# One NeuronCore, attention and two feed-forward layers: the order of 3,095 planned operations read from a table

## The chip, the core and the metric

The kernel runs on one core of a Trainium2 chip. The metric is the device time of one execution in microseconds (us); lower is better. The engines go by the names of the profile: PE is TensorE's matmuls, PEld its weight loads, DVE is VectorE, ACT is ScalarE, POOL is GpSimd, SP is SyncE, which here only issues transfers (DMAs). Each engine runs its own instructions in order, and waits on semaphores for the others.

## What is computed

Attention with rotary positions over 2 batches, 8 heads, 576 positions and 64 channels; its output (1152 tokens of 512) goes through a layer of width 2048 and then through four experts of width 1024 that are all computed and mixed by given probabilities.

```python
q_rot, k_rot = rotate(q), rotate(k)              # per head, 576 x 64
scores = q_rot @ k_rot.T / 8; scores -= max
attn = exp(scores); attn /= sum + 1e-9
x = (attn @ v)                                   # as 1152 x 512
h = x @ w_in                                     # 512 x 2048
g = where(h >= 1, h, where(h <= -1, 0, (h + 1)**2 / 4))
x = g @ w_out                                    # 2048 x 512
for e in range(4):
    out += p[:, e:e+1] * (relu(x @ w1[e]) @ w2[e])   # 512 x 1024, 1024 x 512
```

All is in float32. The kernel splits each operand of a product into a high and a low part that TensorE takes fast, and adds three products (high x high, high x low, low x high).

## The kernel before

The kernel first describes its work as *operations*, each of one engine, by calls of `op(engine, ns, prio, fn, reads, writes, bufs, ...)`: `fn` issues the instructions (one to twenty), `reads` and `writes` name what must come before it, `bufs` are the ring buffers that it occupies. Operations get a number in the order in which they are described, 0 to 3094. `Plan.order` then puts them in one sequence, and the kernel issues them in that sequence; the engine's own order is what is left of it when one looks at that engine alone. The compiler's framework derives the semaphores from the data. `order` keeps a model of the time: when each engine is free (`free`), when an operation's inputs are there (`ready`), when a ring has a buffer. `est(o)` is the earliest start of an operation in this model. Before, the next operation is found greedily: on each engine the one with the smallest start, or among those that can start within `ahead` = 42.6 ns of the engine's being free the one with the smallest priority; then the engine that can start first. Priorities are a base by pair and tile plus one offset per kind of operation (`CFG["o"]`). Where the model sees TensorE idle for more than `fill` = 272 ns, up to 190 us, `order` puts *filler* matmuls into the hole (tile `warm`, L1328): products of the identity that nobody reads. Operation 0 is a placeholder: 1000 ns of TensorE in the model, with no instruction.

**Attention** goes through eight *pairs* of heads, n = 0 to 7 (four per batch). For each: k, q and v are loaded by SyncE in three parts each (positions 0 to 255, 256 to 511, and the last 64; tiles `rawk`, `rawq`, `RV`); `rope` rotates k and q in three steps (L981, L985, L989) on VectorE or GpSimd; `split_h` and `split_l` make high and low parts (`hlk`, `hlq`; L1028 is the low part); TensorE transposes them (`pstk`, `pstq`), ScalarE copies them to `K` and `Q`; a transfer makes the copy K2 with its halves exchanged. In the first pair q and k are worked on in segments, and VectorE and ScalarE make K and K2 from transposes of their own (`k_first`, L1085, L1092).

Then nine *tiles* of 128 rows of scores, s = 0 to 8, in `tile_step`: scores into `sc` (L1162, four matmuls; eight for s = 8, L1172), a ring of two PSUM buffers; the maximum `nm` on VectorE (L1179); the exponential `E` on ScalarE (L1184), which frees `sc`; four transposes of E into `pt` (L1197), a ring of three; and a copy of them (`PT`). For each half of the tiles, `tails` transposes the rest (`pu`), `av` multiplies with v (L1273, 20 matmuls in the records), the reciprocal of the sums goes over DRAM to all partitions (`r`, `rb`, `rt`, `rdram`, `rbs`), and the product `avx` is split into `XH` and `XL`.

**The first layer** (phases 2 and 1) has four *chunks* c of 512 columns, each with three blocks b of 384 tokens and four units: `in_unit` (PSUM tile `pi`, L520) with its activation, and `out_unit` (`po`, L574). The first units of chunk 0 may run within attention. Its weights come in 1 MB blocks of 64-bit numbers (`wrawa`, L378) and are converted on ScalarE and VectorE (`w_split`, L423 to L438, one quarter of a block at a time; later `w_split2`). **The experts** (eight chunks; `in2`, L776; `out2`, L813) follow, with converted weights (`conv1`, `conv2`).

Of the kernel before, what the change touches and what calls it, by code (L numbers as in the profile page):

```python
# [41 lines left out]
    },  # L42
}


def _f32_of_bits(b):
# [90 lines left out]
class Plan:  # L137
# [38 lines left out]
    def order(self):  # L176
        prio = {o: o.prio for o in self.ops}
        free, ready, left = {}, {}, {}
        for o in self.ops:
            free.setdefault(o.eng, self.START.get(o.eng, 0.0))  # L180
            ready.setdefault(o.eng, [])
            left[o.phase] = left.get(o.phase, 0) + 1
            if o.need == 0:
                ready[o.eng].append(o)
        out = []
        n = len(self.ops)
        ahead = CFG["ahead"]

        cols = [0.0] * 1000
        heat, heat_to = CFG["fill"], CFG["fill_to"]  # L190
        port = [0.0, None]
        mode = [0]
        queue = 0.0

        def est(o):
            t = max(free[o.eng], o.ready)
            if o.port:
                t = max(t, port[0])
            if o.phase == 1 and left.get(0, 0):
                return None  # L200
            for b in o.bufs:
                if b.slot is None:
                    r = b.ring
                    if r.ordered and b.idx != len(r.live):
                        return None
                    i = len(r.live) - r.bufs
                    if i >= 0:
                        if r.live[i].left:
                            return None
                        t = max(t, r.live[i].end)  # L210
            if o.eng == "PE" and o.mode != mode[0]:
                t += self.ENTER if o.mode else self.LEAVE
            return t

        while len(out) < n:
            best = None
            for e, rl in ready.items():
                c = None
                for o in rl:
                    t = est(o)  # L220
                    if t is None:
                        continue
                    key = (max(t, free[e] + ahead), prio[o], o.seq)
                    if c is None or key < c[0]:
                        c = (key, t, o)
                if c and (best is None or (c[1], c[0][1]) < (best[1], best[0][1])):
                    best = c
            if best is None:
                raise RuntimeError("no order")
            _, t, o = best  # L230
            if o.eng == "PE" and heat and t - free["PE"] > heat and free["PE"] < heat_to:
                g0 = free["PE"]
                early = g0 < CFG["warm_to"]
                r = self.filler[early]
                i = len(r.live) - r.bufs
                ok = i < 0 or not r.live[i].left
                if ok and i >= 0:
                    g0 = max(g0, r.live[i].end)
                k = int(g0 // self.TICK)
                cyc = 228.0 if g0 < CFG["warm_to"] or cols[k - 1] >= self.FULL else 430.0  # L240
                if CFG["rule"] and g0 > CFG["warm_to"]:
                    ok = ok and cols[k] + CFG["rule"] * (self.TICK * (k + 1) - g0) < self.FULL
                cnt = int((t - g0 - 40) // cyc)
                slow = 0
                if k == 0:
                    slow = min(12, int((t - g0 - 40) // 430.0))
                    cnt = slow + int((t - g0 - 40 - slow * 430.0) // cyc)
                if ok and cnt > 0:
                    f = self.fill(cnt, early)
                    b = f.bufs[0]  # L250
                    b.slot = len(r.live)
                    r.live.append(b)
                    f.start, f.ns = g0, cnt * cyc + slow * (430.0 - cyc)
                    b.end, b.left = g0 + f.ns + (0.0 if early else self.LAT["PE"]), 0
                    for z in range(cnt):
                        at = g0 + z * cyc + min(z, slow) * (430.0 - cyc)
                        cols[int(at // self.TICK)] += 512
                    free["PE"] = g0 + f.ns
                    out.append(f)
                    n += 1  # L260
                    continue
            ready[o.eng].remove(o)
            left[o.phase] -= 1
            o.start = t
            ns = o.ns
            if o.eng == "PE":
                if t > free["PE"] + 20 and o.mode == mode[0] and ns:
                    ns += self.STALL
                mode[0] = o.mode
                k = int(t // self.TICK)  # L270
                if k == 0 or cols[k - 1] < self.FULL:
                    ns *= 1.96
                m = min(1.0, (self.TICK * (k + 1) - t) / ns)
                cols[k] += o.cols * m
                cols[k + 1] += o.cols * (1 - m)
            end = t + ns
            lat = o.lat
            if o.dma:
                queue = max(queue + o.dma, end + lat)
                lat = queue - end  # L280
            free[o.eng] = end
            if o.port:
                x = port[1]
                o.behind = x if x is not None and o.eng == "POOL" and x.eng == "DVE" else None
                port[:] = end, o
            for b in o.bufs:
                if b.slot is None:
                    b.slot = len(b.ring.live)
                    b.ring.live.append(b)
                b.left -= 1  # L290
                b.end = max(b.end, end + lat + self.LAT[o.eng])
            for x in o.outs:
                x.need -= 1
                x.ready = max(x.ready, end + lat + (130.0 if x.eng == o.eng and o.eng != "PE" else
                                                      0.0 if x.eng == o.eng else self.LAT[o.eng]))
                if x.need == 0:
                    ready[x.eng].append(x)
            out.append(o)
        return out
# [1216 lines left out]
```

## Time and profile before

| | us |
|---|---|
| median of 3 runs (lowest, highest) | 745.22 (745.02, 747.79) |
| the profiled execution | 743.66 |
| its span, first to last instruction | 741.9 |
| PE busy in the span | 731.7 |
| DVE busy | 537.3 |
| ACT busy | 352.4 |
| POOL busy | 90.7 |

The profile is of one execution. Busy time is the time in which at least one instruction of an engine runs; for TensorE the ends of matmuls are modelled and successive ones overlap, so that a busy TensorE need not be at its peak. Idle time is followed back to the instruction or transfer that ended it. The profiled execution's own time holds 1.8 us outside its span.

### The profile page before, as it was taken

Reading aid. Unit: us, or ns where it says so; the run is one execution under the profiler, and the core shown is the slowest. Engines: PE = TensorE matmul, PEld = TensorE weight load, DVE = VectorE, ACT = ScalarE, POOL = GpSimd, SP = SyncE. Lnnn points to the kernel's source line nnn. Section 1 sums busy time; section 2 is a strip of 40 time slices with the busy share of each in tenths; the row PEclk is TensorE's granted clock in tenths of the full one; section 3 lists DMA queues with packets and bytes.
Section 4 is the critical chain, followed back from the end, with each engine's and each line's share of the span. In section 5 each row is a group of like instructions: output and inputs, shape, how many; then the busy total and the mean of one; then the engine's idle time right before and its main releaser. Section 6 shows DMA issues by size and latency. Waiting matters only on the chain.

```text
span 741.9 us, 11798 instructions
## 1 busy us (share of the span) xinstructions
PE 731.7 (99%) x4551; PEld 664.1 (90%) x4551; DVE 537.3 (72%) x1054; ACT 352.4 (48%) x801; POOL 90.7 (12%) x88
## 2 busy tenths in 40 slices
PE   8999999999999999999999999999999999999998
PEld 6877778879999999999998889998899989999896
DVE  6789899799999943225898586684866749668462
ACT  4887788776776554435533332331433314333110
POOL 2874433000000021222300000000000000000000
PEclk9999999999999999999999999999999999999999
DMA  6344434223362400000103110111011110111002
GB/s 185 93 118 129 125 98 141 90 74 123 121 215 83 151 0 1 1 2 1 57 1 114 57 47 11 58 57 57 12 46 57 57 57 18 41 58 57 1 29 100
DMA packets 38872, 50.86 MB, mean 69 GB/s; under 512 B 7640, under 2 KB 22560, under 8 KB 38816
## 3 DMA queue, kind: packets, MB, share of 16 engines
q1 hardware_dynamic: 38126, 49.61, 21.4%
q8 instruction: 36, 0.59, 0.3%
q10 hardware_dynamic: 690, 0.49, 0.2%
q14 instruction: 20, 0.16, 0.1%
HBM read 43.34 MB, written 2.40 MB: 62 GB/s over the span
## 4 chain that ended last, share of the span: by engine, by line
PE 90%; DVE 4%; ACT 2%; DMA 2%; POOL 1%; issue 1%; SPq 0%; DVEq 0%; POOLq 0%
PE po L813 27%; PE q L776 23%; PE po L574 13%; PE pi L520 13%; PE av L1273 5%; PE sc L1162 4%; PE pt L1197 3%; ACT E L1184 1%; PE sc L1172 1%; DVE nm L1179 1%; DMA rawq<-in_q_dram 1%; PE pu L1223 1%; DVE tsa L785 1%; DMA rawk<-in_k_dram 1%; PE pstk L1045 1%
## 5 line engine op out<-in xcount | busy, mean ns | idle before, releaser
L785 DVE TENSOR_TENSOR tsa<-q,tsa 128x256 f32<-128x256 f32 (+1 forms) x224 | 93.3, 448 | 32.9 <-PE q L776 32.4
L813 PE MATMUL po<-w,ct 128*128 128x512 f32 (+1 forms) x328 | 99.1, 384 | 0.0
L828 DVE SCALAR_TENSOR_TENSOR ACC<-po,ptile,ACC 128x512 f32<-128x512 f32 (+1 forms) x64 | 46.8, 739 | 65.8 <-PE po L813 65.8
L813 PE MATMUL po<-w,hid1h 128*128 128x512 f32 x256 | 79.0, 390 | 0.0
L813 PEld LDWEIGHTS po<-w,ct 128*128 128x128 f32 x328 | 60.5, 188 | 11.7
L813 PE MATMUL po<-w,tsb 128*128 128x512 f32 (+1 forms) x164 | 63.0, 384 | 0.0
L1184 ACT ACTIVATE E<-sc,nm 128x576 f32<-128x576 f32 x72 | 53.7, 748 | 13.1 <-DVE nm L1179 9.6
L1179 DVE TENSOR_REDUCE nm<-sc 128x1 f32<-128x576 f32 x72 | 52.6, 751 | 8.8 <-PE sc L1162 3.8
L813 PEld LDWEIGHTS po<-w,hid1h 128*128 128x128 f32 x256 | 47.6, 188 | 9.4
L665 ACT CAST w<-wrawa 128x512 fp32r<-128x512 f32 x32 | 18.4, 617 | 67.5 <-PE po L813 63.3
L813 PE MATMUL po<-w,hid1l 128*128 128x512 f32 x128 | 50.0, 390 | 0.0
L541 ACT ACTIVATE hb<-pi,half_t 128x384 f32<-128x384 f32 x48 | 27.8, 578 | 46.3 <-PE pi L520 46.2
L759 ACT ACTIVATE ct<-tsa 128x320 fp32r<-128x320 f32 x64 | 28.9, 471 | 42.7 <-DVE tsa L785 42.7
L1162 PE MATMUL sc<-K,Q 128*128 128x288 f32 x256 | 46.3, 311 | 2.3 <-ACT E L1184 2.1
L545 DVE SCALAR_TENSOR_TENSOR hb<-hb,pi 128x384 f32<-128x384 f32 x48 | 26.3, 550 | 28.0 <-ACT hb L543 17.9
L759 ACT ACTIVATE hid1h<-tsa 128x256 fp32r<-128x256 f32 x64 | 25.4, 418 | 36.8 <-DVE tsa L785 36.7
L1162 PEld LDWEIGHTS sc<-K,Q 128*128 128x128 f32 x256 | 35.9, 188 | 7.6 <-ACT E L1184 5.7
L1197 PE MATMUL pt<-ident,E 128*128 128x128 f32 x288 | 38.4, 274 | 0.3 <-ACT K L1050 0.3
L788 ACT COPY tsa<-q 128x256 f32<-128x256 f32 (+1 forms) x32 | 12.7, 398 | 51.7 <-PE q L776 51.6
L586 DVE TENSOR_TENSOR ACC<-po,ACC 128x384 f32<-128x384 f32 x36 | 20.0, 555 | 23.9 <-PE po L574 23.9
L813 PEld LDWEIGHTS po<-w,tsb 128*128 128x128 f32 x164 | 30.8, 188 | 6.2
L776 PE MATMUL q<-XH,w00l 128*128 128x256 f32 (+1 forms) x120 | 35.5, 296 | 0.0
(234 smaller groups left out, 1961.2 us busy)
## 6 DMA issues: line engine op xcount, KB each, us to landing
wrawa<-in_moe_w_dram SPq DMA_DIRECT2D x16, 1024.0 KB, 5.9
wrawa<-in_moe_w_in_dram SPq DMA_DIRECT2D x5, 1024.0 KB
wrawa<-in_moe_w_out_dram SPq DMA_DIRECT2D x5, 1024.0 KB, 5.1
K<-K SPq DMA_DIRECT2D x14, 304.0 KB, 3.4
ta<-in_moe_w_in_dram SPq DMA_DIRECT2D x3, 1024.0 KB
ta<-in_moe_w_out_dram SPq DMA_DIRECT2D x3, 1024.0 KB, 4.9
rawk<-in_k_dram SPq DMA_DIRECT2D x16, 128.0 KB, 3.6
RV<-in_v_dram SPq DMA_DIRECT2D x16, 128.0 KB, 2.4
```

The costliest lines, as they stand in the source:

```text
L520: nc.tensor.matmul(ps()[:, 0:384], w[:, kt * P:(kt + 1) * P], x[:, kt, cols], start=(kt == 0 and m == 0), stop=(kt == 3 and m == 2))
L574: nc.tensor.matmul(ps()[:, 0:N], lh, rh, start=(kt == 0 and m == 0), stop=(kt == 3 and m == 2))
L759: op("ACT", act_ns(n, port) + 20, pr, lambda: nc.scalar.activation(hv(0), src(), AF.Relu), rk + gates[0], [hk], bufs, phase=1)
L776: nc.tensor.matmul(ps()[:, 0:n], w[x][:, kt, a * P:(a + 1) * P], r[y][:, kt, :], start=(kt == 0 and m == 0), stop=(kt == 1 and m == 2))
L785: nc.vector.tensor_tensor(ct(a, j), psv(), ct(a, i), op=ALU.add)
L813: nc.tensor.matmul(ps()[:, 0:f1 - f0], x[y], w[z][:, f0:f1], start=(kt == 0 and m == 0), stop=(kt == 3 and m == 2))
L828: op("DVE", 65 + 1.17 * (f1 - f0), pr, lambda acc=acc, ps=ps, t=t, f0=f0, f1=f1: nc.vector.scalar_tensor_tensor(acc(), ps()[:, 0:f1 - f0], ...
L1162: nc.tensor.matmul(sc()[:, a, 0:288], lh, KK()[:, c0:c0 + 288], start=(x == 0), stop=(x == 1))
L1179: op("DVE", 665, g0 + O["max"], lambda: nc.vector.tensor_reduce(nm(), pv(), axis=AX.XY, op=ALU.max, negate=True), [sc], [nm], [sc, nm])
L1184: nc.scalar.activation(Et()[:, o0:o0 + 576].rearrange("p (a c) -> p a c", a=2), pv(), AF.Exp, bias=nm(), scale=1.0, accum_out=sm()[:, s:s ...
L1197: nc.tensor.transpose(ps()[:, t * P:(t + 1) * P], Et()[:, c0 + t * P:c0 + (t + 1) * P], ident)
L1273: nc.tensor.matmul(pa()[64 * j:64 * j + 64, 0:N], lh, rh, start=(t == 0), stop=(t == 4))
```

## The change

The greedy choice is replaced by a table, `ORDER`: all 3,095 numbers in the sequence in which they are to be issued. `order` takes the first number that is left, asks `est` for its start, and goes on as before: fillers are still put in where its model sees a hole. `est` gets one more rule: a GpSimd operation that follows a VectorE operation on their shared port starts one VectorE latency (125 ns) later. Nothing else is changed: the offsets stay in the file and have no effect on the sequence any more.

To read the first numbers: 1, 2 and 9 are SyncE's loads of pair 0's k (last 64 positions, first part, second part), 10 its load of q's second part; 3 and 4 load the rotation tables on ScalarE's queue, 5 and 6 parts of q; 45, 46 and 47 are the three rotation steps of k's second segment, 48 to 50 those of q's; 14 to 16 those of k's first; 57 is VectorE's copy to K2 of its second segment; 58 is the split of q's second segment on ScalarE; 868 is the load of the first weight block (1 MB); 133, 134 and 135 load pair 1's k; 142 and 143 are two rotation steps of it on VectorE, 144 the third on GpSimd; 148 and 149 its high and low part; 152, 156 and 162 its transposes; 62, 67, 72 the scores of tiles 0, 1 and 3 of pair 0 (the third to be computed is tile 3), 63 the maximum of tile 0.

```diff
--- before.py
+++ after.py
+ORDER = """
+3 9 45 4 10 1 48 46 49 6 2 47 15 14 5 37 38 51 50 16 18 17 39 19 20 53 58 12 868 7 59 54 40 22 41 23 28 133 8 134 135
+142 143 11 21 144 55 32 24 29 52 33 31 25 136 26 56 30 27 60 138 61 57 137 62 148 42 44 149 145 146 34 238 63 35 36 67
+0 68 43 162 64 72 152 139 69 163 77 73 156 153 65 74 157 78 158 239 240 82 247 75 79 83 147 76 242 66 87 84 150 248 88
+151 243 241 250 80 110 111 85 86 81 92 112 70 108 89 166 93 113 97 13 71 94 109 114 98 154 343 164 159 102 155 90 99
+160 161 167 251 165 116 91 103 141 252 344 168 104 123 105 120 249 253 124 121 254 169 172 115 125 126 100 177 173 347
+174 345 122 257 101 178 261 258 95 353 346 263 262 179 127 348 352 182 267 268 175 271 449 176 448 96 183 255 256 170
+187 106 184 171 107 185 180 213 192 117 188 189 186 181 197 128 356 214 354 259 264 265 269 193 118 140 355 198 357
+260 129 358 451 215 450 194 266 199 216 217 270 119 912 359 869 452 130 202 195 196 203 458 218 207 204 190 208 209
+372 219 220 362 272 870 913 363 373 457 273 228 191 221 210 459 225 131 453 226 205 229 366 227 274 277 206 368 555
+360 367 230 278 554 282 283 361 231 279 211 200 275 212 222 284 276 201 287 374 375 364 244 365 292 871 288 369 371
...
+3065 3063 3066 3064 3067 3068 3071 3069 3072 3070 3073 3074 3077 3075 3078 3076 3079 3080 3083 3081 3084 3085 3082
+3086 3089 3087 3090 3088 3091 3092 3093 3094
+"""
@@ -189,13 +318,15 @@
         cols = [0.0] * 1000
         heat, heat_to = CFG["fill"], CFG["fill_to"]
         port = [0.0, None]
+        table = [self.ops[int(x)] for x in ORDER.split()]
         mode = [0]
         queue = 0.0
 
         def est(o):
             t = max(free[o.eng], o.ready)
             if o.port:
-                t = max(t, port[0])
+                behind = port[1] is not None and o.eng == "POOL" and port[1].eng == "DVE"
+                t = max(t, port[0] + (self.LAT["DVE"] if behind else 0.0))
             if o.phase == 1 and left.get(0, 0):
                 return None
             for b in o.bufs:
@@ -214,7 +345,10 @@
 
         while len(out) < n:
             best = None
-            for e, rl in ready.items():
+            if table:
+                o = table[0]
+                best = (None, est(o), o)
+            for e, rl in ready.items() if best is None else ():
                 c = None
                 for o in rl:
                     t = est(o)
@@ -260,6 +394,8 @@
                     n += 1
                     continue
             ready[o.eng].remove(o)
+            if table:
+                table.pop(0)
             left[o.phase] -= 1
             o.start = t
             ns = o.ns
```

## Rows read from the trace of the kernel before

**Rows 1.** Windows of the whole span: start:end, length, then each engine's busy us (instructions).

```profile
0.00:10.47 10.47, 8.27 (x25) 6.26 (x25) 5.47 (x17) 3.35 (x6) 1.82 (x13) 1.00 0.57 154
...
10.47:172.00 161.53, 157.12 (x1204) 126.23 (x1205) 139.23 (x281) 125.86 (x353) 62.87 (x49) 1.00 0.39 112
...
172.00:735.50 563.50, 563.27 (x3300) 528.82 (x3299) 390.83 (x755) 223.24 (x443) 25.96 (x26) 1.00 0.16 54
```

**Rows 2.** Groups by line on PE, 0 to 172 us: count, busy, mean ns, idle before.

```profile
L1328 PE MATMUL warm<-identr 128*128 128x512 f32 x40 | 13.4, 474 | 2.0 <-DVE identr L1314 2.0
```

**Rows 3.** Chain that ended last: start us, us, what, count.

```profile
43.75 2.84 PE av L1273 x20
...
47.86 0.53 PE sc L1162 x4
...
49.66 2.31 PE av L1273 x20
...
99.84 1.31 PE pt L1197 x12
...
180.22 8.32 PE po L574 x48
```

**Rows 4.** Waits of PE: total us, times, longest us.

```profile
PE sc L1162 <- ACT E L1184: 2.1, 5, 0.6
```

**Rows 5.** Timeline, 51.8 to 56.2 us: start, us, what, in brackets idle before and releaser.

```profile
52.37 1.58 PE L1162 MATMUL sc<-K,Q 128*128 128x288 f32 x8
...
53.59 1.42 DVE L1179 TENSOR_REDUCE nm<-sc 128x1 f32<-128x576 f32 x2
...
54.39 0.74 ACT L1184 ACTIVATE E<-sc,nm 128x576 f32<-128x576 f32 x1 [0.26 <-DVE nm L1179]
...
55.27 0.80 PE L1162 MATMUL sc<-K,Q 128*128 128x288 f32 x4 [0.43 <-ACT E L1184]
```

**Rows 6.** Timeline of the start, by engine: queues SPq and ACT, then DVE, POOL, PE.

```profile
0.74 0.70 SPq L896 DMA_DIRECT2D rawk<-in_k_dram  x1
...
1.50 0.93 SPq L890 DMA_DIRECT2D rawk<-in_k_dram  x2
...
10.41 0.46 SPq L378 DMA_DIRECT2D wrawa<-in_moe_w_in_dram  x1
...
4.56 1.28 ACT L945 ACT_TABLE_LOAD   x1 [4.56 <-DMA tabs<-in_tab_dram]
...
5.58 0.49 DVE L981 TENSOR_TENSOR ta<-rawk,tabs 128x320 f32<-128x320 f32 x1 [3.65 <-DMA rawk<-in_k_dram]
...
11.68 0.68 DVE L1092 CAST K<-pstk(5, 1)_187 128x512 fp32r<-128x512 f32 x1
...
13.40 0.76 DVE L985 TENSOR_TENSOR ta<-rawk,tabs 128x576 f32<-128x576 f32 x1 [0.37 <-DMA rawk<-in_k_dram]
...
14.98 1.42 POOL L989 TENSOR_TENSOR ta<-ta 128x576 f32<-128x576 f32 x1 [12.37 <-DVE ta L981]
...
16.89 1.41 DVE L1179 TENSOR_REDUCE nm<-sc 128x1 f32<-128x576 f32 x2
...
18.59 0.97 PE L1045 MATMUL pstk<-identr,hlk 128*128 128x128 f32 x9 [0.50 <-POOL hlk L1028]
...
19.40 1.29 PE L1162 MATMUL sc<-K,Q 128*128 128x288 f32 x8
```

**Rows 7.** Window 172 to 222 us as in Rows 1, and timeline around its end.

```profile
172.00:222.00 50.00, 50.00 (x290) 50.00 (x289) 48.36 (x70) 37.18 (x64) 0.00 (x0) 1.00 0.50 162
...
220.40 0.55 DVE L549 TENSOR_TENSOR ha<-hb,ha 128x384 fp32r<-128x384 f32 x1
...
221.70 1.55 PE L574 MATMUL po<-ha,w 128*128 128x384 f32 x8
```

**Rows 8.** Window 12 to 15 us: the last two columns are DMA share and GB/s.

```profile
12.00:15.00 3.00, 2.81 (x21) 2.09 (x21) 2.63 (x6) 2.48 (x10) 0.02 (x1) 1.00 0.98 329
```

**Rows 9.** Groups by line on DVE, 20 to 172 us: one of a conversion's.

```profile
L425 DVE SCALAR_TENSOR_TENSOR hb<-wrawa,hb 128x512 uint32<-128x512 uint32 x8 | 5.5, 694 | 0.3
```

113 rows, old and new, of the table ORDER are left out of this document.

## Prediction

> **What bounds the kernel now.** I read the busy shares of the page first: TensorE is busy for 731.7 us of the span of 741.9, so the question is what it is busy with and where it waits. The windows by stage answer the second half. From 172 us, where attention ends, to 735.5 us it is idle for 563.50 - 563.27 = 0.2 us, and what follows is the last stores; from 10.47 us (the first real transpose) to 172 us it is idle for 161.53 - 157.12 = 4.4 us [rows 1]. Not all of the busy time is work. The planner puts filler matmuls into holes that it foresees: 40 of them, 13.4 us [rows 2]. The first 25 take 8.27 us before 10.47 us [rows 1], so 15 fillers and 13.4 - 8.3 = 5.1 us stand among real work. The feed-forward part streams: 48 matmuls of 384 columns take 8.32 us, 173 ns each, one block behind the other [rows 3]. An order can win nothing there. What it can win is at most 4.4 + 5.1 = 9.5 us in attention, and what an earlier first transpose gives.
>
> Next, who releases TensorE. The longest sum of waits is that of the scores for the exponential [rows 4]. The timeline shows why. Scores have two buffers, so tile s+2 waits until tile s has been through VectorE's maximum (0.75 us) and ScalarE's exponential (0.74 us). The scores of two tiles run as one piece (eight matmuls from 52.37, the first four done at about 53.1), the maxima from 53.59, the first exponential 54.39 to 55.13, and the next scores at 55.27, after 0.43 us of idle TensorE [rows 5]. From the end of the scores' streaming to the next use of the buffer, the least that I find between rows is 0.04 + 0.75 + 0.04 + 0.74 + 0.14 and 0.16 us for the tail of the matmuls: 1.87 us. TensorE must have that much other work between tile s and tile s+2, or it waits.
>
> **The change, part by part.** *What stays.* The operations, tiles and buffers are the same. I compared the table with the order that before's own rule gives, engine by engine. From TensorE's 386th operation on (of 1144; it runs at 237 us in this trace) the two agree, and on the other engines from 250 us on: the last two thirds of the span keep their order, and cost nothing.
>
> *The start.* Before, VectorE's first rotation waits until 5.58 for k rows whose load was SyncE's second (issued at 1.50); from there it works without a break for 7.4 us, up to the wait of 0.37 us that ends at 13.40 [rows 6]. The table puts the rows that are rotated first at the head of SyncE's queue (0.74), so I start VectorE at 4.9, and add 0.3 us for q rows that are wanted second. The same 7.4 us of work follows, less the 0.6 us of a copy of K2 (11.68) that the table moves behind it: 4.9 + 0.3 + 7.4 - 0.6 = 12.0. Then come pair 1's two rotations, at 12.0 instead of 13.40 where they waited 0.37 us for their load; GpSimd's addition, at 14.98 before, begins at 13.5; VectorE's split of k, which waits for it (16.40 before), at 14.9; GpSimd's own split of the same length 1.42 us comes behind that and ends at 16.9. VectorE's split of k stands in front of the first maximum in both orders, 16.89 before. In the table the first scores end near 14.9 (the K2 copies follow the rotations at 13.4), and the maximum starts behind the split at 15.35. Exponential 16.1 to 16.85, so the third tile's scores can start at 17.0, where pair 1's k transposes, which wait for GpSimd's split, are also ready. Before, those transposes began at 18.59 after 0.50 us of idle, and the third tile's scores at 19.40 [rows 6]. Term: 19.4 - 17.05 = **-2.3 us**. Its bounds are 0 (the load comes late, below) and -2.5.
>
> *ScalarE's table load.* It starts at 4.56, when the load awaited by the first ScalarE operation lands, and takes 1.28 us [rows 6]. In the table the first ScalarE operation is a split of q, ready at about 8.7, so the load would run there and end near 10.0, and the split at 10.4. VectorE comes to the subtraction that needs it at about 10.7. Cost nothing, covered by VectorE's own 5 us of rotations; without that cover 0.3 us.
>
> *The scores' spacing.* I added up TensorE's work between every tile's scores and those two tiles on, for all 70 such spans, with the durations of the chain (scores 0.53, four transposes of E 0.44, av 2.31 and 2.84) [rows 3]; the rest is small. In the order of before 20 spans are below 1.87 us and are short by 5.9 us together; that agrees with what idle time and fillers show. In the table 9 are, short by 2.5 us. Before, scores of two tiles stand side by side 19 times, in the table 5 times. Term: **-3.4 us**. Were the round trip 2.2 us, as it is where a copy stands in a queue, the sums would be 13.1 and 7.2, and the term -5.9; with half of the shortfall hidden it would be -1.7. I keep -3.4, since 1.87 is what the rows with a wait show.
>
> *New places.* In the table the transposes of tile 2 of pair 0 follow its scores after 1.50 us of other work, 0.37 short of the same round trip: **+0.4 us**. Of the 4.4 us of idle time [rows 1] the wait for the exponential is 2.1 [rows 4]; 2.3 us have other causes (the sums' reciprocals, copies, the normalised output). In the table such neighbours go in some places and come in others: 0, with -1 and +1.5 as bounds.
>
> *The end of attention.* From the last av to the first output unit of the second chunk TensorE has 50 us of work and VectorE 45.2 us; VectorE's last piece begins at 220.40 and ends at 220.95, and TensorE wants it at 221.70 [rows 7]. VectorE is busy 48.4 of these 50 us, so it is late next. In the table four operations of TensorE are moved ahead of the last av: 47.9 us against VectorE's 45.8 us, with the normalisation first in line where it stood 2 us back. I take 0, and up to +1 us as bound.
>
> **Sum:** -2.3 - 3.4 + 0.4 = -5.3 us, all of it before 172 us. The profiled execution took 743.66 us, 1.56 us below the median of 745.22; so 738.4 for a profile, and 739.9 against the median.
>
> **Rivals.** *The weight load comes in the way.* The table sends the first weight block (1 MB) ahead of pair 1's k rows; before, it was issued at 10.41, behind them [rows 6]. From 12 to 15 us, where that block moves, the queues carry 329 GB/s at 98% [rows 8]: 3.2 us for 1 MB. If the k rows land that much later, the start gains nothing and loses 0.9 us: -5.3 + 3.2 = -2.1, or 743.1. Against it: the block is issued near 3.4 instead of 10.4, and the rows are wanted at 12.0. The Trainium skill ("DMA: Bandwidth & Descriptors", HWDGE ordering) says that each of the 16 DMA engines takes descriptors of one issuing queue in ring order; by that rule the rows cannot start before the block is through, and this rival is what it would do if the block were still moving at 9.
>
> *VectorE takes over.* If its idle time after 172 us doubles (1.64 us more), the first output unit of chunk 2 waits for it, and if other new waits take their +1.5: -5.3 + 1.6 + 1.5 = -2.2, or 743.0. For it: VectorE is already busy 139.2 of the 161.5 us of attention [rows 1].
>
> *Slower: a conversion in front of a maximum.* The longest instruction of a weight's conversion takes 0.69 us on VectorE [rows 9], and it stands in a group of up to three: at most 2.1 us. VectorE works in order. In the table a conversion stands right before a maximum 7 times (6 before). Each that holds back scores which are already there costs up to 2.1 us, all seven 14.7: -5.3 + 14.7 = +9.4, or 754.6. To be slower by 3.7 us it takes 9.0 us, five of the seven with nothing hidden. Against it: the same neighbours exist now.
>
> *The order does not matter.* TensorE's work is the same, and the waits only change their names: 745.2.
>
> **How the numbers follow.** A measurement of this kernel can tell about 0.5%, 3.7 us. My forecast (a gain over 3.7, 736 to 741.5) gets 0.62; the late load 0.13, VectorE 0.12 and no change 0.06, all within 0.5%: 0.31; slower 0.07. Predicted time 739.9. The range reaches from -9.2 us, near the 9.5 that waits and fillers hold together, to just over the no-change case: 736 to 746.
>
> **What would show it.** Right: attention ends near 166.5 instead of 171.7; the third tile's scores start near 17; the wait of scores for the exponential falls under 1 us; fewer than 40 fillers; from there on blocks of 8.32 us as before. Wrong: pair 1's k rows land after 12.5; a new wait of output units for VectorE near 216; TensorE's granted clock below 1.00 between 10 and 172 us, because fewer fillers stand in the holes.

## The result

| | us |
|---|---|
| before, median of 6 runs (lowest, highest) | 745.29 (744.57, 747.79) |
| after, median of 6 runs (lowest, highest) | 739.33 (738.39, 739.46) |
| ratio after / before, 95% interval | 0.9918 [0.9904, 0.9931] |
| profiled execution before / after | 743.66 / 739.46 |
| span before / after | 741.9 / 737.7 |

The change gains 6.0 us by the medians, 4.2 by the two profiles: the profiled execution of before is as fast as any that was timed (743.7 to 747.2 beside the first experiments), so the traces explain 4.2 us, and the rest only in kind.

The windows of after, as in [rows 1]; the line numbers of after are 136 higher.

```profile
0.00:10.47 10.47, 8.49 (x28) 6.83 (x29) 4.86 (x14) 1.69 (x2) 1.83 (x13) 1.00 0.66 206
10.47:166.00 155.53, 151.94 (x1187) 125.48 (x1186) 139.60 (x277) 126.44 (x355) 62.42 (x49) 1.00 0.41 112
...
172.00:735.00 563.00, 562.15 (x3301) 527.68 (x3299) 390.04 (x753) 219.87 (x437) 25.97 (x26) 1.00 0.16 54
```

Of the 0.85 us that TensorE is idle behind 172 us, 0.62 lie behind its last matmul.

The fillers of after, by line, as in [rows 2], and TensorE's waits from 10.47 to 175 us, as in [rows 4]:

```profile
L1464 PE MATMUL warm<-identr 128*128 128x512 f32 x38 | 11.3, 462 | 2.0 <-DVE identr L1450 2.0
```

```profile
PE sc L1298 <- ACT E L1320: 1.2, 2, 1.0
PE pstk L1181 <- POOL hlk L1164: 1.1, 1, 1.1
PE pstq L1181 <- ACT K L1228: 0.4, 1, 0.4
PE rb L1385 <- DVE r L1383: 0.4, 1, 0.4
```

The five waits of scores for the exponential have become two, one of 1.0 us. To see where the time went, both traces need the same cuts. Windows of before:

```profile
10.47:24.00 13.53, 12.75 (x87) 10.25 (x88) 9.29 (x20) 9.94 (x28) 8.31 (x6) 1.00 0.62 176
24.00:52.00 28.00, 27.15 (x218) 21.91 (x217) 23.92 (x47) 21.99 (x67) 20.75 (x17) 1.00 0.39 105
52.00:94.00 42.00, 39.74 (x308) 31.44 (x308) 36.98 (x77) 32.59 (x92) 19.98 (x16) 1.00 0.47 128
```

and of after:

```profile
10.47:24.00 13.53, 11.85 (x86) 9.80 (x84) 11.37 (x25) 10.61 (x31) 7.26 (x6) 1.00 0.35 94
24.00:52.00 28.00, 26.43 (x213) 21.44 (x214) 23.60 (x43) 22.01 (x66) 18.84 (x15) 1.00 0.45 113
52.00:94.00 42.00, 41.87 (x338) 34.11 (x338) 40.24 (x81) 34.90 (x99) 21.33 (x17) 1.00 0.53 139
```

From 52 to 94 us (pairs 2 to 4) TensorE is idle for 2.26 us before and for 0.13 after, and does 30 matmuls more in the same time; up to 52 us after is the idler one, but before's busy time there holds 15 fillers. A second reading agrees: I summed TensorE's real matmuls (without fillers) in both traces and compared the times at which the same sum is reached. After is ahead by -1.7 us at its first transpose, -0.3 at 19 us, +1.5 at 39, 0.0 at 52, +1.2 at 70, +3.7 at 94, +4.1 at 166, and +4.0 to +4.2 from there to the end. This *lead* is used for all runs below.

The idle time explains 2.1 of the 3.7 us; most of the rest hides under the modelled ends of matmuls. Measured *from start to start* of neighbouring matmuls, less what such a pair usually takes, before has five waits of 0.44 to 0.70 us between 52 and 94 us and three of 0.24, 3.5 us together; after has one of 0.30. The profile shows about 0.16 us less of each as idle time.

The timeline of after at the place of [rows 5]:

```profile
52.73 0.76 PE L1298 MATMUL sc<-K,Q 128*128 128x288 f32 x4
...
53.43 0.80 PE L1298 MATMUL sc<-K,Q 128*128 128x288 f32 x4
...
54.07 1.63 PE L1333 MATMUL pt<-ident,E 128*128 128x128 f32 x12
...
55.51 0.79 PE L1298 MATMUL sc<-K,Q 128*128 128x288 f32 x4
```

The same round trip runs, but 1.6 us of transposes stand between the second scores and the third, and nothing waits. The start, as in [rows 6]:

```profile
1.73 0.68 SPq L1032 DMA_DIRECT2D rawk<-in_k_dram  x1
...
3.57 1.28 ACT L1137 ACT_TABLE_LOAD   x1 [3.57 <-issue]
4.10 0.43 DVE L1117 TENSOR_TENSOR ta<-rawk,tabs 128x256 f32<-128x256 f32 x1 [2.17 <-DMA rawk<-in_k_dram]
4.22 0.47 SPq L514 DMA_DIRECT2D wrawa<-in_moe_w_in_dram  x1
8.05 0.49 DVE L1121 TENSOR_TENSOR ta<-rawk,tabs 128x320 f32<-128x320 f32 x1 [1.97 <-DMA rawk<-in_k_dram]
8.46 0.48 DVE L1117 TENSOR_TENSOR ta<-rawk,tabs 128x320 f32<-128x320 f32 x1
8.97 0.88 SPq L1026 DMA_DIRECT2D rawk<-in_k_dram  x2
13.69 0.76 DVE L1117 TENSOR_TENSOR ta<-rawk,tabs 128x576 f32<-128x576 f32 x1 [0.45 <-ACT hlk_first L1142]
15.27 1.42 POOL L1125 TENSOR_TENSOR ta<-ta 128x576 f32<-128x576 f32 x1 [12.65 <-DVE ta L1121]
17.16 1.42 DVE L1315 TENSOR_REDUCE nm<-sc 128x1 f32<-128x576 f32 x2
18.85 0.28 PE L1181 MATMUL pstk<-identr,hlk 128*128 128x128 f32 x1 [1.07 <-POOL hlk L1164]
18.96 0.76 PE L1298 MATMUL sc<-K,Q 128*128 128x288 f32 x4
```

VectorE starts 1.48 us earlier than before and then stands still for 1.97 us. The first maximum is at 17.16 (16.89 before) and the third tile's scores at 18.96 (19.40 before). Pair 1's k rows are loaded into the same buffer as pair 0's (`rawk` is a ring of one), so their first load goes out at 8.97, when VectorE has read it for the last time (8.46 + 0.48 = 8.94).

### The profile page after: what moved, and what is told of

It is laid out like the page before. It is cut to its first block, busy times and chain, and to the rows that moved or that the text cites. A ratio compares the mean times of both kernels' runs of the same rounds, so it can differ in the third digit from the quotient of the medians.

```text
span 737.7 us, 11822 instructions
## 1 busy us (share of the span) xinstructions
PE 728.6 (99%) x4549; PEld 664.2 (90%) x4549; DVE 540.3 (73%) x1054; ACT 351.7 (48%) x801; POOL 90.2 (12%) x88
## 4 chain that ended last, share of the span: by engine, by line
PE 89%; DVE 3%; DMA 3%; ACT 2%; SPq 1%; issue 1%; POOL 1%; DVEq 0%; POOLq 0%
PE po L949 27%; PE q L912 23%; PE pi L656 14%; PE po L710 14%; PE av L1409 4%; PE sc L1298 3%; PE pt L1333 3%; DMA rawk<-in_k_dram 1%; PE sc L1308 1%; ACT E L1320 1%; DMA rbs<-rdram 1%; DMA rdram<-rt 1%; SPq L1026 1%; DVE tsa L921 1%; DVE nm L1315 1%
## 5 line engine op out<-in xcount | busy, mean ns | idle before, releaser
L1298 PE MATMUL sc<-K,Q 128*128 128x288 f32 x256 | 48.8, 315 | 1.3 <-ACT E L1320 1.2
L1333 PE MATMUL pt<-ident,E 128*128 128x128 f32 x288 | 40.5, 275 | 0.2
```

The costliest lines, as they stand in the source:

```text
L1298: nc.tensor.matmul(sc()[:, a, 0:288], lh, KK()[:, c0:c0 + 288], start=(x == 0), stop=(x == 1))
L1333: nc.tensor.transpose(ps()[:, t * P:(t + 1) * P], Et()[:, c0 + t * P:c0 + (t + 1) * P], ident)
```

## The experiments

Each change of the order is shown by operation numbers. The median of before on the same chip stands beside each time, then the ratio to it with its interval; versions that ran on different chips are compared by these ratios, in us of 745.

### Is it the order at all, and which part of it?

*table_of_before*: before's own sequence, written into the table.

```diff
 ORDER = """
-3 9 45 4 10 1 48 46 49 6 2 47 15 14 5 37
+0 3 1 4 2 9 5 10 6 139 7 140 141 11 14 12
 ...
```

> The changed kernel with the order of the kernel before written into its table; what is left of the change is the port rule of the model, which now only moves fillers. If the order is the cause, the time is that of before, 744.5 to 746.2 us, with 36 to 42 fillers. Rival, the port rule and the fillers are the cause: 742 us or less.

Measured: 745.26 (before 745.52), 0.9994 [0.9984, 1.0004]. The new rule in `est` and the new loop give nothing; the sequence does.

*start_only* and *rest_only*: the table up to operation 207 (pair 1's last scores, about 47 us) and before's sequence behind it, and the other way round. *late_only*: before's sequence up to pair 4's last scores (about 95 us), then the table.

```diff
 # start_only
 202 195 196 203 458 218 207
-204 190 208 209 372 219 220 362
+190 191 870 204 453 913 219 244
 # rest_only
-203 458 218 207
+453 218 913 219 207
+357 359 130 195 196 208 209 372
 # late_only
+... 768 445 510 506 518 522
+519 515 587 511 516 687 677 523
```

> The table up to the last scores of pair 1 (operation 207, at 47 us), then the order of before for all that is left. If the gain comes after 47 us, the time is 744.3 to 745.8 us, since the lead of the changed kernel over before is 0.0 us at that point. Rival, the early start that I forecast: 742 us or less.

> The order of before up to the last scores of pair 1 (47 us), then the table's order for all that is left. If the gain comes after 47 us, it has nearly all of it: 739.0 to 741.3 us. Rival, the early start: 743.5 us or more.

> The order of before up to the last scores of pair 4 (about 95 us), then the table's. Theory (the gain is made in pairs 2 to 4, nothing behind them): the lead at 94 us is about 0, at 166 us at most 0.7 (the two waits of 0.38 and 0.42 us that the order of before has behind 94), 744.5 to 745.3. Rival (some of the gain is made in the second half of the attention, where the table puts other work between the scores too): 742.5 to 743.5.

Measured: start_only 747.14, 1.0024 [1.0014, 1.0033]; rest_only 741.43, 0.9952 [0.9937, 0.9968] (both beside 745.52); late_only 744.85 (before 745.39), 0.9996 [0.9987, 1.0004]. Behind 95 us nothing is gained: late_only came out as the theory said. The two halves at 47 us do not add up: +1.8 and -3.6 make -1.8, the whole makes -6.1. At the seam of start_only TensorE loses 1.57 us from start to start at 48.35 (between a transpose of tile 4 and pair 2's first scores, which wait for the exponential); in rest_only's profiled execution (744.90, its slowest) 1.74 us at 49.03, where transposes of k wait for GpSimd. An order cut at one place leaves work on the other engines that the next part expects done.

### Is it the spacing of the scores?

*side_by_side* takes the spacing of five scores out of the table; *spread_before* puts spacing into before's sequence and moves nothing else; *pe_before* brings TensorE's sequence in pairs 2 to 4 as near to before's as the other engines' order allows: 10 of its 89 operations there stand elsewhere than before, and of the six places with two scores side by side two are still apart. In the first and the last version a few operations of VectorE and ScalarE had to follow. TensorE's sequence (sc scores, pt, pu, pstk transposes, rb the sums' transposes):

```diff
 # side_by_side, against the table
-sc2_1 rb11 sc2_2 ... sc2_6 pt2_4 pt2_3 pt2_1 sc2_7 ... sc2_8 pt2_5 pstk4_8 pstk4_0 sc3_0
+sc2_1 sc2_2 rb11 ... sc2_6 sc2_7 pt2_4 pt2_3 pt2_1 ... sc2_8 sc3_0 pt2_5 pstk4_8 pstk4_0
-sc3_4 rb30 pu3_0 sc3_5 ... sc4_4 pt4_2 pt4_0 sc4_5
+sc3_4 sc3_5 rb30 pu3_0 ... sc4_4 sc4_5 pt4_2 pt4_0
 # spread_before, against before
-sc2_1 sc2_2 pt1_6 ... sc2_6 sc2_7 pt2_0 pt2_1 ... sc2_8 sc3_0 pstk4_0 pstk4_4
+sc2_1 pt1_6 sc2_2 ... sc2_6 pt2_0 pt2_1 sc2_7 ... sc2_8 pstk4_0 pstk4_4 sc3_0
-sc3_4 sc3_5 pt3_1 ... sc3_8 sc4_0 pstk5_0 ... sc4_4 sc4_5 pt4_0
+sc3_4 pt3_1 sc3_5 ... sc3_8 pstk5_0 sc4_0 ... sc4_4 pt4_0 sc4_5
 # pe_before, against the table: sc2_0 to sc4_8 nearly as before, other engines nearly as in the table
```

> The table of the change with five scores of pairs 2 to 4 put directly behind the scores ahead of them (2_2 behind 2_1, 2_7 behind 2_6, pair 3's first behind 2_8, 3_5 behind 3_4, 4_5 behind 4_4), as they stood in the order before; the transposes and other work that stood between come behind. The other engines' orders stay, but for two operations each of VectorE and ScalarE. Theory (the spacing of the scores is what gains): each of the five gives TensorE a wait of 0.4 to 0.7 us back, at the second score or at the one that follows, 2.0 to 3.5 us in all, 741.3 to 742.8. Rival (the spacing is a by-product, and VectorE's and ScalarE's orders gain): TensorE waits at one place and makes it up at the next, 739.3 to 740.3. Second rival (TensorE's order fits the other engines' orders and any change to it alone costs more than the spacing): over 743.

> The order of before, with six scores moved behind one or two pieces of TensorE's own work that followed them (2_2 behind a transpose, 2_7 behind two, pair 3's first behind two transposes of k, 3_5, 4_5 and pair 4's first behind one); no other engine's order changes, and none of the rest. Theory (spacing alone gains, whatever the other engines do): the waits of 0.50 to 0.70 us at 54.57, 57.55, 81.89, 89.45 and 93.18 shrink by half or more, 742.5 to 744. Rival (the engines that take the scores and the transposes off keep the old order, so the moved work waits for them in turn): 745 to 747.

> The table of the change, but TensorE takes the operations of pairs 2 to 4 (from pair 2's first scores to pair 5's first) in the order that it had before, in which two scores mostly stand side by side; the other engines keep the table's order but for the few operations that have to follow. Theory (the scores' spacing in these pairs is where the gain is made): TensorE's waits of 0.4 to 0.7 us ahead of the second of two scores are back, about six of them, the lead over the kernel before grows by no more than 1 us between 52 and 94 us in place of 3.7, and the time is 742 to 743.5. Rival (the gain comes from the other engines' order, and TensorE's order follows it): 739.3 to 740.3.

Measured: side_by_side 742.85 (before 744.74), 0.9971 [0.9962, 0.998]: 3.9 us slower than the change (3.5 by the medians), with an interval clear of the change's. The theory had 2.0 to 3.5. Its lead is +1.4 at 62 us, -1.4 at 70 and +0.3 at the end. Of the 3.7 us that it ends behind the change's, 2.6 are lost by 70 us, where two of the five moves lie; timeline of side_by_side:

```profile
60.97 0.77 PE L1298 MATMUL sc<-K,Q 128*128 128x288 f32 x4
...
61.83 0.74 ACT L1320 ACTIVATE E<-sc,nm 128x576 f32<-128x576 f32 x1 [0.71 <-DVE nm L1315]
...
62.71 0.80 PE L1298 MATMUL sc<-K,Q 128*128 128x288 f32 x4 [0.97 <-ACT E L1320]
...
67.64 0.79 PE L1298 MATMUL sc<-K,Q 128*128 128x288 f32 x4 [0.57 <-ACT E L1320]
```

Scores 2_7, pulled in front of three transposes, wait 0.97 us for the exponential that frees their buffer; pair 3's first wait 0.57; two waits of 0.30 stand between and behind them. The other three moves show no wait over 0.3 us. What is lost behind 70 us is not traced to a move; one new wait there is of 0.66 us, for a reciprocal at 165.15. So it is shown that scores put side by side wait for the exponential, at two of five places. That the spacing by itself is worth 3.9 us is not: the second rival, by which any change to TensorE's order alone costs that much, stands. By the ratio the time is 743.1 where before is at 745.3, which is over the rival's 743, and pe_before below speaks for it.

spread_before: 745.04 (before 744.74), 1.0008 [0.9999, 1.0017]. Its rival was right: spacing alone gives nothing in the old order. Of the five waits (from start to start; in order of time three are of scores for the exponential, one is of transposes for a copy of K, one of the sums' transpose for a reciprocal) those at 54.57, 57.55 and 89.45 are gone or under 0.4 us, that at 81.89 stays (0.64), that at 93.18 grows to 1.37, and a new one comes. Timeline of spread_before, the new one and the grown one:

```profile
54.29 0.63 PE L1333 MATMUL pt<-ident,E 128*128 128x128 f32 x4 [0.82 <-DVE PU L1279]
...
95.03 0.27 PE L1385 MATMUL rb<-ident,r 128*5 128x128 f32 x1 [1.21 <-DVE r L1383]
```

The transpose moved in front of the scores waits 0.82 us for a buffer that VectorE empties in its old place, and the sums' transpose waits 1.21 us for a reciprocal that VectorE still does behind two copies (0.43 us before).

pe_before: 751.95 (before 745.39), 1.0084 [1.0069, 1.0099]. Both of its expectations failed: 12.4 us slower than the change and 6.3 slower than before. Window of pe_before:

```profile
52.00:94.00 42.00, 36.27 (x279) 27.51 (x276) 32.32 (x65) 28.35 (x79) 17.18 (x15) 1.00 0.46 115
```

TensorE is idle there for 42.0 - 36.27 = 5.7 us, and its waits for the exponential in the whole of attention make 5.7 us in eight places. TensorE's nearly old sequence with the others' new one is worse than either whole.

### What eats the lead at 40 us?

In the change a lead of 1.5 us at 39 us is 0.0 at 43. Timeline of after:

```profile
37.33 1.60 POOL L1117 TENSOR_TENSOR ta<-rawk,tabs 128x576 f32<-128x576 f32 x1
37.58 1.40 DVE L1153 CAST hlq<-ta 128x64 fp32r<-128x64 f32 x1
...
39.23 0.74 DVE L1315 TENSOR_REDUCE nm<-sc 128x1 f32<-128x576 f32 x1
...
40.01 0.74 ACT L1320 ACTIVATE E<-sc,nm 128x576 f32<-128x576 f32 x1 [1.18 <-DVE nm L1315]
...
40.89 0.80 PE L1298 MATMUL sc<-K,Q 128*128 128x288 f32 x4 [1.04 <-ACT E L1320]
```

A cast of 64 columns takes 1.40 us, and ends 0.05 us after GpSimd's operation beside it. *no_collision* moves that operation of GpSimd behind the next:

```diff
 # GpSimd's sequence
-353 352 256
+353 256 352
```

> The table of the change with one operation of GpSimd moved: its sum of two products (operation 352) comes behind the subtraction 256 instead of ahead of it, so that it no longer runs from 37.33 to 38.93 us beside VectorE's short cast of 64 columns, which took 1.40 us there and about 0.19 elsewhere. Theory (the two engines keep each other out, and the maximum, the exponential and the scores behind the cast are late by that): the cast is back at 0.2 to 0.5 us, the maximum of pair 1's fifth tile ends near 38, and TensorE's lost 1.20 us at 39.56 are gone or under 0.4; if that lead is carried to the end, 738.1. Rival (VectorE's other work has room behind it, or the collision moves to the next pair of operations): the cast is short but the lead is gone again by 60 us, 739.3; or GpSimd's later subtraction delays the transposes of pair 2, 740.

Measured: 739.96 (before 745.39), 0.9934 [0.992, 0.9948]: no gain. Timeline of no_collision:

```profile
37.70 0.19 DVE L1153 CAST hlq<-ta 128x64 fp32r<-128x64 f32 x1
...
42.20 1.45 POOL L1125 TENSOR_TENSOR ta<-ta 128x576 f32<-128x576 f32 x1
42.31 1.96 DVE L1117 TENSOR_TENSOR ta<-rawq,tabs 128x576 f32<-128x576 f32 x1
...
44.19 0.74 DVE L1315 TENSOR_REDUCE nm<-sc 128x1 f32<-128x576 f32 x1
...
45.83 0.27 PE L1385 MATMUL rb<-ident,r 128*4 128x128 f32 x1 [1.15 <-DVE r L1383]
```

The cast is back at 0.19 us and TensorE's loss at 39.56 is gone, but now a rotation that takes 0.74 us in after takes 1.96 beside GpSimd's next operation, and the sums' transpose behind it waits 1.15 us (0.40 in after). The mechanism is shown; the collision only moved, as the rival had it.

### What holds the start?

*w_late* moves the 1 MB weight load (868) and a load of v (12) behind pair 1's k rows; *k_first* and *k4_first* change the order of the first small loads; *start_all* joins k4_first and w_late and takes the fillers behind 15 us away.

```diff
 # SyncE's queue: table, w_late, k_first, k4_first, start_all
-9 10 1 2 12 868 133 134 135
+9 10 1 2 133 134 135 12 868
+9 2 1 10 12 868 133 134 135
+1 9 2 10 12 868 133 134 135
+1 9 2 10 133 134 135 12 868
 # VectorE, in the last three
-45 48 46 49 47 15 14
+45 46 47 15 14 48 49
 # start_all
-"fill_to": 190000.0
+"fill_to": 15000.0
```

> The table with two numbers moved: the first weight block (1 MB) and one load of v go behind pair 1's k loads in SyncE's queue. If the weight block holds up pair 0's k rows, VectorE's idle time of 1.97 us before 8.05 falls under 0.8 us and the scores of the third tile start near 17.6 instead of 18.96. Carried to the end that is 737.6 to 738.4 us. Rival, the waits near 40 to 45 us take the lead away again: third tile early, but 739.0 to 739.8 us. Second rival, the k rows are late for another reason: VectorE still idles 1.5 us or more there.

> The table of the change with k's first four blocks (operation 2) second instead of fourth in SyncE's queue, and VectorE's rotations of them ahead of q's. Theory A (the order of the small first loads costs VectorE its 1.97 us of idle time up to 8.05, but the third tile's scores are set by pair 1: the first maximum stands on VectorE behind the cast of pair 1's rows, which waits for GpSimd's sum, which waits for pair 1's rows at 13.7): the rotations of k's first rows start near 6, the first transposes come near 11.2 instead of 12.2, and still the first maximum starts at 17.1 and the third tile's scores at 18.9; 739.3, within 0.4. Theory B (the start term as the forecast had it: what VectorE saves ahead of the first transposes reaches the third tile): the third tile's scores near 17.8, and 738.2 if it is carried to the end.

> The table of the change with SyncE's 32 KB load of k's fifth block (operation 1) first, as it was before, then 9, 2 and 10, and VectorE's rotations of k ahead of q's. In the run with k's 128 KB second, VectorE still stood idle until 8.10, since the rotation also reads this 32 KB load, which was third in both. Theory A (that small load, issued at 1.73 in place of 0.74, is what VectorE waits for): VectorE starts near 4.8 in place of 4.1, its idle of 1.97 us is under 0.5, and the first transposes come 1 to 1.5 us earlier, near 11; the third tile's scores stay at 18.5 to 19, since pair 1's rows at 13.7 set them, and the time at 739.0 to 739.6. Theory B (the start reaches the third tile): scores of the third tile at 17.5 to 18 and 738.2 to 738.6. Rival (the bytes of all first loads together set the landing): VectorE idles until 7.5 or later.

> The run with k's fifth block first, and besides, the 1 MB weight block and one load of v moved behind pair 1's k rows in SyncE's queue, and no filler matmuls after 15 us (with the weights late alone, a run of 2.77 us of fillers stood at 23.56 while a transpose's data were ready about 24.1). Theory (pair 1's k rows set the first maximum once the first tile is early): the rotation of pair 1's k starts by 12.6 in place of 13.69, the third tile's scores by 17.9 in place of 18.96, no loss of over 1.5 us at 23 to 26; carried to the end 738.0 to 738.6, the fastest of all. Rival (the lead of the start is eaten at 36 to 46 us as in the change itself): third tile early, time 739 to 739.8. Rival (the weight conversions come late and hold the attention's other work, fillers or not): 740.5 or more.

Measured: w_late 741.62 (before 745.52), 0.9946 [0.9934, 0.9958]; k_first 739.38 (before 745.39), 0.9921 [0.9906, 0.9935]; k4_first 739.03 and start_all 739.52 (both beside 744.74), 0.9923 [0.9909, 0.9936] and 0.9934 [0.9921, 0.9946]. None can be told from the change but w_late, which is slower.

In w_late VectorE still stands idle for 2.33 us, to 8.38, though the weights go out at 11.34: they do not hold pair 0's rows up. The rotation at 8.05 reads two loads: operation 2, the first 128 KB of k, and operation 1, the 32 KB of its last positions. In k_first VectorE idles 2.47 us, to 8.10, with operation 2 second in the queue: there it waited for operation 1, issued third. In the change and in w_late, operation 2 stands behind operation 1 and is late with it: by the packets in w_late's trace operation 1 had moved by 6.8 us and operation 2 by 7.5. With operation 1 first, both have moved by about 4.7 us, and the idle time in front of this rotation is gone. Timeline of k4_first:

```profile
5.36 0.43 DVE L1117 TENSOR_TENSOR ta<-rawk,tabs 128x256 f32<-128x256 f32 x1 [3.43 <-DMA rawk<-in_k_dram]
...
6.57 0.49 DVE L1121 TENSOR_TENSOR ta<-rawk,tabs 128x320 f32<-128x320 f32 x1
...
10.81 0.41 DVE L1164 TENSOR_TENSOR hlk_first<-ta,hlk_first 128x256 fp32r<-128x256 f32 x1
...
12.70 0.46 PE L1221 MATMUL pstk(5, 0)_181<-identr,hlk_first 128*128 128x128 f32 x4
...
13.59 0.76 DVE L1117 TENSOR_TENSOR ta<-rawk,tabs 128x576 f32<-128x576 f32 x1 [1.16 <-DMA rawk<-in_k_dram]
```

Theory A holds but for the first transposes: they were to come near 11 and came at 12.70. Their data are there at 10.81 + 0.41 = 11.22, as in the planner's model, which starts them at 11.12; but TensorE is inside a run of fillers. The model lets that run begin at 0; in the trace it begins at 1.99, when the identity that it multiplies is ready, and ends about that much later. VectorE then waits 1.16 us for pair 1's rows, at 13.59, and these set the third tile's scores (18.88), as theory A has it. In start_all those rows are early; timeline of start_all:

```profile
11.74 1.30 PE L1464 MATMUL warm<-identr 128*128 128x512 f32 x5
...
12.44 0.75 DVE L1117 TENSOR_TENSOR ta<-rawk,tabs 128x576 f32<-128x576 f32 x1
12.88 0.46 PE L1221 MATMUL pstk(5, 0)_179<-identr,hlk_first 128*128 128x128 f32 x4
...
14.77 0.29 DVE L1228 CAST K<-pstk(4, 0)_215 128x128 fp32r<-128x128 f32 x1 [0.92 <-PE pstk(4, 0)_215 L1221]
```

The rotation is at 12.44, but now VectorE waits 0.92 us for TensorE's transposes, which stood behind fillers until 12.88. The third tile's scores start at 18.72 (18.88 in k4_first, 18.76 in w_late, 19.14 in k_first), far from the 17.9 that was expected. The time is in the range of the first rival, but not for its reason: the lead, 1.6 us at 39, is still 1.3 at 43 and 4.5 at 250, 0.5 more than the change's. The profiled execution, the slowest of start_all, then loses 1.3 us at 531.57, in the experts, where TensorE waits 0.94 us for VectorE in an order that is the same in all versions; whether the other executions do is not known. Each hold that was taken away uncovered the next. A start without these fillers was not tried.

w_late loses 2.1 us to fillers as well. Its timeline:

```profile
23.34 0.74 ACT L1320 ACTIVATE E<-sc,nm 128x576 f32<-128x576 f32 x1 [0.34 <-DVE nm L1315]
23.56 2.77 PE L1464 MATMUL warm<-identr 128*128 128x512 f32 x11
...
26.17 0.60 PE L1333 MATMUL pt<-ident,E 128*128 128x128 f32 x4
```

The exponential is done at 24.08, and its transposes start at 26.17, behind 11 fillers. Here too the data come when the model says (24.10), and the fillers begin late, at 23.56 where the model has 21.57. The lead at 24.5 us is -1.9 in w_late; in start_all, where no filler stands there, it is +0.5.

## Why the prediction was right, and where it was not

**What bounds the kernel.** Right: nothing changed behind attention (0.2 us of waits for VectorE behind 172 us in both traces), and 3.7 us of the lead are there at 94 us.

**The scores' spacing, -3.4.** Right in its mechanism: the waits between 52 and 94 us are gone, and the lead grows there by 3.7 us. That the sizes agree is in part luck. Counted again pair by pair, with the same durations and the planner's own for the rest, the shortfall falls by 2.8 us, and only 0.8 of that lies in pairs 2 to 4; 1.5 lie in pairs 0 and 1, 0.5 in pair 5. At 19 to 39 us the trace does show a lead that grows by 1.8 us, but it is lost again at 40; in pairs 2 to 4 the waits were longer than a round trip of 1.87 us makes them. With the prediction's other value, 2.2 us, the count gives these pairs 2.2. What it could not see at all is that spacing is worth something only with the other engines' order to match: alone, in the old order, it gave nothing (1.0008). The term prices the whole table, not the moves of the scores in it.

**The start, -2.3.** This step failed; it measured 19.40 - 18.96 = -0.4. The step's words are that VectorE starts at 4.9 and that "the same 7.4 us of work follows". It started at 4.10 and idled 1.97 us, with the 32 KB load third in the queue instead of first (issued at 1.73 instead of 0.74) and 128 KB of k behind it; k4_first, which puts the 32 KB first, has no such idle time. The forecast had looked at the rows rotated first and not at all rows that the rotation of k's first segment reads. So pair 1's rotation began 1.7 us late (13.69 for 12.0), and from there the forecast's chain held: each step came 1.7 to 2.0 us late (GpSimd's addition 15.27 for 13.5, the first maximum 17.16 for 15.35, the third tile's scores 18.96 for 17.0). Behind it stood two more limits, as k4_first and start_all showed: pair 1's rows at 13.6, which the forecast had as a rival, and fillers in front of the first transposes, which it did not name. At 52 us the lead is 0.0: the start gives no measurable part of the gain.

**Table load, new places, end of attention.** ScalarE's table load ran at 3.57, not at 8.7; it cost nothing, as said. The new place (+0.4) does not show: between 19 and 39 us TensorE loses nothing over 0.3 us. New waits came within the bounds of -1 to +1.5, at 40 us, by a collision that no row of before had suggested. From 167.6 to 217.6 us TensorE is busy for all of the 50.00 us and VectorE for 49.46: the cover held, with less room than in [rows 7].

**Rivals.** The weight load does come in the way, and by the rival's own condition: issued at 4.22, it lands 7.4 us later, so it is still moving at 9. Pair 1's rows are there at 13.59 in k4_first, issued from 7.49, and before 12.44 in start_all, where they go first. But what it costs was hidden behind the rest of the start. VectorE did not take over; a conversion held a maximum back by 1.1 us at most (that of 68.35), and TensorE did not wait for it; and the order does matter.

**The signs.** The fillers (38, under 40) and the blocks of 8.32 us behind attention came as they were to. The third tile's scores start at 18.96 and not near 17, the waits of scores for the exponential are 1.2 us and not under 1, and the last av ends at 169.7 and not near 166.5, though in part because other work was moved ahead of it. One sign of being wrong came: pair 1's rows land after 12.5. The other two did not: there is no new wait near 216 us, and the granted clock stays at 1.00.

**The sum.** -5.3 was forecast; -4.2 measured between the profiles and -6.0 between the medians. The sum lies between by luck as well: the start gave 1.9 us less than its term. The 738.4 for a profile was missed by 1.1 us; the 739.9 against the median came within 0.6, because the medians differ by 1.8 us more than the profiles, which no term foresaw. The table's executions lie within 1.1 us (738.39 to 739.46), those of before within 3.5 (743.66 to 747.21): the difference between 4.2 and 6.0 lies in how far a typical execution of the old order falls behind its best. Which waits grow in it was seen once only: table_of_before's profile, 745.30 us with the old order, is 0.8 us behind the profile of before at 19 us, 1.8 at 70 and no more at 166.

None of the versions tried is faster than the change by what the measurement can tell; k4_first (0.9923) is its equal.

## What to carry to other kernels

Where a two-buffer ring sets the pace, add up the other work between an entry and the next but one, and compare it with the round trip; but move the other engines' work with it, since each takes its own in order, and half of a reordering can be slower than none. Before counting on an earlier start, list every load that the second and third instruction read, and what the engine after them does meanwhile: filler work that is counted by a model holds an in-order engine when the engine comes to it later than the model says, even if the data are on time. A removed wait is worth what the next limit leaves of it: no_collision, k4_first and start_all each took a real wait away and gained nothing.

## What the runs showed of the hardware

A GpSimd operation can hold up a VectorE operation for its whole length: the 64-column cast took 1.40 us beside a GpSimd operation and 0.19 without it, the 576-column rotation 1.96 instead of 0.74. Each ended 0.05 to 0.62 us after the GpSimd operation that had begun 0.11 to 0.25 us ahead of it. The Trainium skill ("SBUF — State Buffer", Who interferes with whom) says that the two engines share one pair of ports as an exclusive lock: a VectorE instruction in a two-port mode, which a cast can enter, contends for it with GpSimd, the one that issues first holds it for its whole instruction and the other blocks; an instruction with two inputs in SBUF contends as well. These traces agree.

In k_first a load of 32 KB issued third, at 1.73 us, let VectorE wait until 8.1 us; issued first, at 0.74, it was there with the others by 6.6 us in k4_first. Why it lands so late when it is third, and with it what stands behind it, is open.

Behind the first transpose the change has 3 fillers where before had 15, and TensorE's granted clock was 1.00, its level of 2.4 GHz, in every window of both: there the fewer fillers cost no clock.
